# A chunk's products with itself: three split products on the whole array, or float32 products in its four quarters, with one output copied ahead of a cast

## The chip, the cores and the metric

One Trainium2 chip, one core of it. The metric is the device time of one execution in microseconds (us), lower is better. The kernel before took 387.55 us (median of 3 runs, 386.8 to 387.71).

## The reference, cut to what matters

```python
# x (8, 4224, 192), weight (8 heads, 7 taps): a causal convolution in time, heads of 24 channels
w = softmax(weight, axis=-1)
x = sum over k of w[h, k] * x[b, s - 6 + k, head h]       # per head of 24 channels
# then, on its result x, with w_val, w_out (192, 192) and conv_w (5, 192)
gate = sigmoid(sum over k of conv_w[k] * x[b, s - 4 + k])  # per channel
val = x @ w_val
out = (gate * val) @ w_out                                 # float32
```

## The kernel before, in words

Channels lie on the partitions, time along the free axis. The 8 sequences are laid end to end in two streams of four. Of 192 channels 128 form chunk 1 and 64 form chunk 2. Chunk 1 has a plane for each stream (`x1`, two planes of 128 partitions); chunk 2 of both streams shares one plane (`x2`: stream 0 on partitions 0 to 63, stream 1 on 64 to 127). A stream's time is cut into 14 groups and these into 37 steps (`STEPS`): two of 288 columns, six of 432, 27 of 482, and at the end one of 500 and one of 244. A step holds both streams, so its planes have 482 columns each.

**Stage 1, the first convolution** (`conv_unit`, L303). TensorE multiplies windows of `x` with a band matrix of the softmax weights, as float32 products of 64 by 64 (or 56) with 58 columns, four beside each other in the four quarters of the array (L319). Two PSUM outputs `pc` of a unit are copied by ScalarE to `e` (L330), and DMAs of SyncE's queue scatter `e` into `x1` and `x2` (L359). A group has six units in the main part, made two groups ahead, two units a step (`todo`).

**Stage 2, the gate.** ScalarE opens it with the first tap (`gate_open`, L393), VectorE adds four taps (`gate_taps`, L400), ScalarE closes with a sigmoid (`gate_close`, L413); in two parts: A is chunk 1 (`pa`, `g1`), B chunk 2 (`pb`, `g2`).

**Stage 3, the value projection, and stage 4, the output projection.** `v` is `x` times `w_val`; VectorE multiplies it into the gate in place (`gated`, L511); `o` is that product times `w_out`, one step later; ScalarE copies `o` to `ot` (`project`, L527), and a DMA writes it out. A plane is split ahead of its products (`split1`, `split2`): ScalarE casts it to a float32r high part (`xh`, `ph`; L421 for chunk 1, L429 for chunk 2), GpSimd subtracts that for the low part (`xl`, `pl`; L422, L430). A split product is three matmuls: high by high, low weight by high, high weight by low. A projection has four kinds of products, by the chunk that goes in and the chunk that comes out:

- `main` (L464): chunk 1 to chunk 1, per stream three split matmuls of 128 by 128.
- `rows` (L477): chunk 2 to chunk 1, split, for each stream in its 64 rows of the array.
- `columns` (L492): chunk 1 to chunk 2, in float32, 128 by 64, a stream in each half of the array's columns, in four pieces of 120 or 121 columns.
- `diagonal` (L454): chunk 2 to chunk 2. Its weight is a 128 by 128 block with the 64 by 64 weight twice on the diagonal (`W22`), so three split matmuls of all 482 columns take both streams.

The outputs are `v_0`, `v_1` (chunk 1, a plane per stream) and `v_2` (chunk 2 of both), and the same of `o`.

**What sets the order.** The engines run in the order in which the code issues (`manual_schedule`). In the main loop (L640) a step n issues on TensorE: `diagonal` of `v` n and of `o` n-1, `main` of `v`, `columns` of `v` and of `o`, `rows` of `v` and of `o`, `main` of `o`, two conv units. VectorE's order is two A taps, `gated` 2, a B tap, `gated` 0, a B tap, `gated` 1, then A, B, A, B. ScalarE's is close and open B, the split of n+1, close and open A, the cast of chunk 2's gated product, the copy of `o_2`, the cast of chunk 1's gated product (`split_gated1`), the copies of `o_0` and `o_1`, the four copies of the conv units. Steps 0 to 3 have a loop of their own (`HEAD`, L579).

**PSUM.** The gate's `pa` and `pb` hold three of the eight banks. The other five rotate (pool `ps`, five buffers): an output gets the bank of the fifth output before it and waits until that is read. With two conv units a step's ten outputs are, in order, `v_2`, `o_2`, `v_0`, `v_1`, `o_0`, `o_1`, `pc` 0 and 1 of the first unit, `pc` 0 and 1 of the second. So the second unit's `pc` 1 waits for the copy of `o_0`, the next step's `v_2` for the copy of `o_1`, and the next `o_2` for the copy of the first unit's `pc` 0.

Of the kernel before, what the change touches and what calls it, by code (L numbers as in the profile page):

```python
# [44 lines left out]
def second(n):  # L45
    return NS * n * WIN - reach(n)
# [24 lines left out]
STEPS = []  # L71
# [34 lines left out]
def kernel(  # L106
# [9 lines left out]
    nc = tc.nc  # L116
# [18 lines left out]
    o = 0  # L135
# [128 lines left out]
    W11, W12, W21, W22 = 0, 128, D, D + 128  # L264
# [24 lines left out]
    w_val, w_out = Weight("wv"), Weight("wo")  # L289
# [3 lines left out]
    HALVES = (slice(0, 64), slice(64, 128))  # L293
# [80 lines left out]
    def views(n, k=KG - 1):  # L374
        g, o, m = STEPS[n]
        b = second(NJS[g])
        x1v = x1s[g][:, : 2 * b].rearrange("p (a t) -> p a t", a=2)
        return x1v[:, :, o + k : o + k + m], x2s[g][:, o + k : o + k + m]
# [3 lines left out]
    accs, g1s, g2s, xs, pr, ots, banks = {}, {}, {}, {}, {}, {}, {}  # L382
# [12 lines left out]
    def gate_taps(n, i, k0=1, k1=KG):  # L395
        if n >= N:
            return
        acc = accs[n, i]
        for k in range(k0, k1):
            nc.vector.scalar_tensor_tensor(  # L400
                out=acc, in0=views(n, k)[i], scalar=cwt[:, i, k : k + 1],
                in1=acc, op0=ALU.mult, op1=ALU.add,
            )

    def gate_close(n, i):
        if n >= N:
            return
        m = STEPS[n][2]
        if i == 0:
            dst = g1s[n] = gp.tile([128, 2, MB], F32, tag="g1", name=f"g1_{n}")[:, :, :m]  # L410
        else:
            dst = g2s[n] = gp.tile([128, MB], F32, tag="g2", name=f"g2_{n}")[:, :m]
        nc.scalar.activation(dst, accs.pop((n, i)), AF.Sigmoid)  # L413
# [3 lines left out]
    def split1(pool, tag, n, x):  # L417
        m = STEPS[n][2]
        h = pool.tile([128, 2, MB], F32R, tag="h", name=f"{tag}h_{n}")[:, :, :m]
        l = pool.tile([128, 2, MB], F32R, tag="l", name=f"{tag}l_{n}")[:, :, :m]  # L420
        nc.scalar.copy(h, x)  # L421
        nc.gpsimd.tensor_tensor(out=l, in0=x, in1=h.bitcast(F32), op=ALU.subtract)  # L422
        return h, l
# [9 lines left out]
    def bank(what, n, q):  # L433
        t = ps.tile([128, 512], F32, tag="p", name=f"{what}_{n}_{q}")[:, : STEPS[n][2]]
        banks[what, n, q] = t
        return t

    def operands(what, n):
        return (w_val, *xs[n, 1], *xs[n, 2]) if what == "v" else (w_out, *pr[n, 1], *pr[n, 2])

    def parts(w, h, l):
        return (w.h, h), (w.l, h), (w.h, l)

    def ok(n):
        return 0 <= n < N

    def diagonal(what, n):
        if not ok(n):
            return
        acc = bank(what, n, 2)  # L450
        w, _, _, h2, l2 = operands(what, n)
        r = slice(W22, W22 + 128)
        for i, (a, b) in enumerate(parts(w, h2, l2)):
            nc.tensor.matmul(acc, lhsT=a[:, r], rhs=b, start=(i == 0), stop=False)  # L454

    def main(what, n, q):
        if not ok(n):
            return
        fresh = (what, n, q) not in banks
        acc = bank(what, n, q) if fresh else banks[what, n, q]  # L460
        w, h, l, _, _ = operands(what, n)
        r = slice(W11, W11 + 128)
        for i, (a, b) in enumerate(parts(w, h, l)):
            nc.tensor.matmul(  # L464
                acc, lhsT=a[:, r], rhs=b[:, q], start=(fresh and i == 0), stop=(not fresh and i == 2)
            )

    def rows(what, n):
        if not ok(n):
            return  # L470
        fresh = (what, n, 0) not in banks
        two = [bank(what, n, q) if fresh else banks[what, n, q] for q in range(2)]
        w, _, _, h2, l2 = operands(what, n)
        r = slice(W21, W21 + 128)
        for i, (a, b) in enumerate(parts(w, h2, l2)):
            for acc, p in zip(two, HALVES):
                nc.tensor.matmul(  # L477
                    acc, lhsT=a[p, r], rhs=b[p], start=(fresh and i == 0), stop=(not fresh and i == 2)
                )

    def columns(what, n):
        if not ok(n):
            return
        m = STEPS[n][2]
        acc = banks[what, n, 2]
        w = w_val if what == "v" else w_out
        x = views(n)[0] if what == "v" else g1s[n]
        cuts = [m * i // 4 for i in range(5)]
        for i in range(4):
            c = slice(cuts[i], cuts[i + 1])  # L490
            for q, p in enumerate(HALVES):
                nc.tensor.matmul(  # L492
                    acc[p, c], lhsT=w.f[:, W12 : W12 + 64], rhs=x[:, q, c],
                    start=False, stop=(i == 3),
                )

    def split(n):
        if n >= N:
            return
        x1, x2 = views(n)  # L500
        if n < 2:
            xs[n, 2] = split2(sp, "x", n, x2)
        xs[n, 1] = split1(sp, "x", n, x1)
        if n >= 2:
            xs[n, 2] = split2(sp, "x", n, x2)

    def gated(n, q):
        if not ok(n):
            return
        v = g1s[n][:, q] if q < 2 else g2s[n]  # L510
        nc.vector.tensor_tensor(out=v, in0=banks.pop(("v", n, q)), in1=v, op=ALU.mult)  # L511

    def split_gated1(n):
        if ok(n):
            pr[n, 1] = split1(pp, "p", n, g1s[n])

    def split_gated2(n):
        if ok(n):
            pr[n, 2] = split2(pp, "p", n, g2s[n])

    def project(n, q):
        if not ok(n):
            return
        m = STEPS[n][2]
        if n not in ots:
            ots[n] = op.tile([128, 3 * MB], F32, tag="ot", name=f"ot_{n}")
        nc.scalar.copy(ots[n][:, q * m : (q + 1) * m], banks.pop(("o", n, q)))  # L527
        o = 3 * sum(s[2] for s in STEPS[:n])
        if n == LAST:
            nc.sync.dma_start(out[:, o + q * m : o + (q + 1) * m], ots[n][:, q * m : (q + 1) * m])  # L530
        elif q == 1:
            nc.sync.dma_start(out[:, o : o + 3 * m], ots[n][:, : 3 * m])
# [9 lines left out]
    def conv(k):  # L542
        for _ in range(k):
            if done[0] < len(units):
                conv_unit(done[0])
                done[0] += 1

    todo = [0] * (N + 1)
    for g in range(LAG, NG):
        a, b = SOON.get(g) or (first[g - LAG], first[g - 1])  # L550
# [27 lines left out]

    for n in range(HEAD):  # L579
        k = 2 if n < 2 else 3  # L580
        diagonal("v", n)
        split(n + 1)
        if n != 1:
            diagonal("o", n - 1)
        main("v", n, 0)
        main("v", n, 1)
        if n == 1:
            diagonal("o", n - 1)
        else:
            gate_taps(n + 1, 0, 1, k)  # L590
        columns("v", n)
        gated(n, 2)
        if n == 1:
            gate_taps(n + 1, 0, 1, k)
        columns("o", n - 1)
        split_gated2(n)
        project(n - 1, 2)
        rows("v", n)
        gated(n, 0)
        gated(n, 1)  # L600
        rows("o", n - 1)
        main("o", n - 1, 0)
        project(n - 1, 0)
        main("o", n - 1, 1)
        project(n - 1, 1)
        conv(1)
        split_gated1(n)
        now = todo[n] if n == 0 else todo[n] // 2
        conv(now - 1)
        gate_taps(n + 1, 0, k, KG)  # L610
        gate_close(n + 1, 0)
        gate_open(n + 2, 0)
        gate_taps(n + 1, 1)
        conv(todo[n] - now)
        gate_close(n + 1, 1)
        gate_open(n + 2, 1)
# [16 lines left out]
    def flush(i):  # L633
        for n, _ in [p for p in pending if p[1] == i]:
            gate_close(n, i)
            gate_open(n + 1, i)
            pending.remove((n, i))

    taps("AA")
    for n in range(HEAD, N + 1):  # L640
        diagonal("v", n)
        flush(1)
        split(n + 1)
        diagonal("o", n - 1)
        main("v", n, 0)
        main("v", n, 1)
        taps("AA")
        columns("v", n)
        gated(n, 2)
        flush(0)  # L650
        taps("B")
        columns("o", n - 1)
        split_gated2(n)
        project(n - 1, 2)
        rows("v", n)
        gated(n, 0)
        taps("B")
        gated(n, 1)
        rows("o", n - 1)
        split_gated1(n)  # L660
        main("o", n - 1, 0)
        taps("ABAB")
        project(n - 1, 0)
        main("o", n - 1, 1)
        project(n - 1, 1)
        conv(todo[n])
# [77 lines left out]
```

## Time and profile before

| | us |
|---|---|
| median of 3 runs | 387.55 |
| the profiled execution | 383.81 |
| its span, first to last instruction | 382.0 |
| TensorE busy in the span | 356.5 |
| VectorE busy | 331.7 |
| ScalarE busy | 327.6 |
| GpSimd busy | 251.1 |
| TensorE's mean granted clock | 0.996 |

The profile's page gives the busy time of each engine over the span; the views of the trace behind it give single instructions with start, duration and, in brackets, the idle time ahead and what ended it. TensorE's recorded durations include the way through the array, so that neighbours overlap: what a matmul costs is the difference of two starts. A float32 product shows as two records, so 8 products stand as x16. Some matmul records are missing. PE is TensorE, ACT ScalarE, DVE VectorE, POOL GpSimd, SP SyncE.

### The profile page before, as it was taken

The page shows a single profiled execution, that of the slowest core. Times are in us where ns is not written, and L with a number is a line of the kernel's source. Part 1 is how long each engine was busy: PE and PEld are TensorE (multiplying, and loading weights), DVE is VectorE, ACT ScalarE, POOL GpSimd, SP SyncE. Part 2 cuts the span into 40 slices and gives each one's busy share as a digit, 9 for nine tenths or more (in the row PEclk, how much of TensorE's full clock was granted, in tenths as well). Part 3 has the DMA queues.
Part 4 walks back from the last instruction along what each step waited for, and adds up shares of the span by engine and source line. Part 5 has one row for each costly group of instructions (what it writes and reads, how often), then busy time and mean ns, then how long its engine had stood idle before and what let it go on. Part 6 is the DMA issues. An engine that isn't in the chain of part 4 may idle for free.

```text
span 382.0 us, 14551 instructions
## 1 busy us (share of the span) xinstructions
PE 356.5 (93%) x6130; PEld 289.1 (76%) x6130; DVE 331.7 (87%) x439; ACT 327.6 (86%) x570; POOL 251.1 (66%) x177
## 2 busy tenths in 40 slices
PE   8798988898999999999999999999999999999895
PEld 7776876787877777777777777777877777776684
DVE  3899889688998988999898898898898899999960
ACT  7589889879998898898898899899899999898863
POOL 1969655556666666666767766666667666677772
PEclk9899999999999999999999999999999999999999
DMA  8888787996986986986986996996898794431224
GB/s 272 232 250 252 223 284 224 257 266 202 277 266 171 258 273 189 238 264 196 243 262 187 205 270 205 232 288 204 203 272 252 177 297 143 140 114 78 79 104 174
DMA packets 38954, 83.30 MB, mean 218 GB/s; under 512 B 4936, under 2 KB 17008, under 8 KB 38888
## 3 DMA queue, kind: packets, MB, share of 16 engines
q1 hardware_dynamic: 37440, 80.64, 71.4%
q0 software_dynamic: 896, 1.27, 1.4%
q8 instruction: 48, 0.79, 0.9%
q10 hardware_dynamic: 552, 0.46, 0.4%
q14 instruction: 18, 0.15, 0.2%
HBM read 30.06 MB, written 26.00 MB: 147 GB/s over the span
## 4 chain that ended last, share of the span: by engine, by line
PE 43%; DVE 14%; ACT 13%; DMA 12%; POOL 9%; issue 5%; SPq 3%; DVEq 0%; ACTq 0%; POOLq 0%
DMA x<-e 11%; PE v L464 8%; DVE g L511 6%; PE pc L319 6%; ACT ph L421 6%; PE v L492 6%; PE v L477 5%; PE o L492 5%; DVE pb L400 5%; PE v L454 5%; PE o L454 4%; POOL pl L422 4%; ACT ot L527 3%; PE o L464 2%; SPq L359 2%
## 5 line engine op out<-in xcount | busy, mean ns | idle before, releaser
L400 DVE SCALAR_TENSOR_TENSOR pa<-x,cwt,pa 128x964 f32<-128x964 f32 (+4 forms) x148 | 173.2, 1170 | 2.3 <-ACT pa L393 0.4
L422 POOL TENSOR_TENSOR xl<-x,xh 128x964 fp32r<-128x964 f32 (+4 forms) x37 | 73.5, 1987 | 81.5 <-ACT xh L421 70.5
L400 DVE SCALAR_TENSOR_TENSOR pb<-x,cwt,pb 128x482 f32<-128x482 f32 (+4 forms) x148 | 102.4, 692 | 0.6
L422 POOL TENSOR_TENSOR pl<-g,ph 128x964 fp32r<-128x964 f32 (+4 forms) x37 | 79.6, 2152 | 29.1 <-ACT ph L421 25.1
L511 DVE TENSOR_TENSOR g<-v,g 128x482 f32<-128x482 f32 (+4 forms) x111 | 69.5, 631 | 32.8 <-PE v L492 20.0
L319 PE MATMUL pc<-band,x 64*56 64x58 f32 (+1 forms) x3776 | 74.4, 220 | 14.7 <-ACT ot L527 9.1
L319 PEld LDWEIGHTS pc<-band,x 64*56 64x56 f32 (+1 forms) x3776 | 65.3, 132 | 28.1 <-ACT ot L527 13.5
L330 ACT COPY e<-pc 120x348 f32<-120x348 f32 (+2 forms) x148 | 59.5, 489 | 5.1 <-PE pc L319 5.1
L527 ACT COPY ot<-o 128x482 f32<-128x482 f32 (+4 forms) x111 | 56.2, 538 | 3.0 <-PE o L464 2.4
L421 ACT CAST ph<-g 128x964 fp32r<-128x964 f32 (+4 forms) x37 | 35.4, 958 | 23.0 <-DVE g L511 22.8
L430 POOL TENSOR_TENSOR pl<-g,ph 128x482 fp32r<-128x482 f32 (+4 forms) x37 | 43.6, 1179 | 2.7 <-ACT ph L429 2.7
L430 POOL TENSOR_TENSOR xl<-x,xh 128x482 fp32r<-128x482 f32 (+4 forms) x37 | 42.0, 1136 | 3.2 <-ACT xh L429 3.1
L393 ACT ACTIVATE pa<-x,cwt 128x964 f32<-128x964 f32 (+4 forms) x37 | 38.1, 1030 | 2.8 <-DMA x<-e 1.7
L492 PEld LDWEIGHTS v<-x,wvf 128*64 128x64 f32 x592 | 29.3, 136 | 11.7 <-issue 10.8
L492 PE MATMUL v<-x,wvf 128*64 128x121 f32 (+5 forms) x592 | 37.4, 267 | 0.0
L492 PE MATMUL o<-g,wof 128*64 128x121 f32 (+5 forms) x592 | 35.5, 261 | 0.0
L413 ACT ACTIVATE g<-pa 128x964 f32<-128x964 f32 (+4 forms) x37 | 34.3, 927 | 1.2 <-DVE pa L400 1.1
L421 ACT CAST xh<-x 128x964 fp32r<-128x964 f32 (+4 forms) x37 | 34.8, 942 | 0.0
L464 PE MATMUL o<-ph,woh 128*128 128x482 f32 (+4 forms) x74 | 31.2, 421 | 0.0
L492 PEld LDWEIGHTS o<-g,wof 128*64 128x64 f32 x592 | 30.8, 136 | 0.1
L464 PE MATMUL v<-xh,wvh 128*128 128x482 f32 (+4 forms) x74 | 27.5, 372 | 1.2 <-ACT e L330 1.2
L464 PE MATMUL o<-pl,woh 128*128 128x482 f32 (+4 forms) x74 | 27.5, 372 | 0.0
(75 smaller groups left out, 568.8 us busy)
## 6 DMA issues: line engine op xcount, KB each, us to landing
x<-xw SPq DMA_DIRECT2D x72, 300.0 KB
out<-ot SPq DMA_DIRECT2D x27, 723.0 KB
x<-e SPq DMA_DIRECT2D x45, 271.9 KB
x<-xw SPq DMA_DIRECT2D x16, 360.0 KB
x<-e SPq DMA_DIRECT2D x36, 135.9 KB
out<-ot SPq DMA_DIRECT2D x6, 648.0 KB
x<-e SPq DMA_DIRECT2D x20, 163.1 KB
x<-e SPq DMA_DIRECT2D x18, 90.6 KB
```

Of the source, the lines that this page charges most:

```text
L319: nc.tensor.matmul(pc[r][c0:c1, k * HW : (k + 1) * HW], lhsT=xtiles[i][p, c + c0 : c + c1], rhs=band[p, 4 * q + hi, :], start=True, stop=True,
L330: nc.scalar.copy(ev[:, a : a + w, r, :], pc[r][:M, : w * HW].rearrange("p (w t) -> p w t", t=HW))
L393: nc.scalar.mul(acc, views(n, 0)[i], cwt[:, i, 0:1])
L400: nc.vector.scalar_tensor_tensor(out=acc, in0=views(n, k)[i], scalar=cwt[:, i, k : k + 1], in1=acc, op0=ALU.mult, op1=ALU.add,)
L421: nc.scalar.copy(h, x)
L422: nc.gpsimd.tensor_tensor(out=l, in0=x, in1=h.bitcast(F32), op=ALU.subtract)
L430: nc.gpsimd.tensor_tensor(out=l, in0=x, in1=h.bitcast(F32), op=ALU.subtract)
L454: nc.tensor.matmul(acc, lhsT=a[:, r], rhs=b, start=(i == 0), stop=False)
L464: nc.tensor.matmul(acc, lhsT=a[:, r], rhs=b[:, q], start=(fresh and i == 0), stop=(not fresh and i == 2))
L492: nc.tensor.matmul(acc[p, c], lhsT=w.f[:, W12 : W12 + 64], rhs=x[:, q, c], start=False, stop=(i == 3),)
L511: nc.vector.tensor_tensor(out=v, in0=banks.pop(("v", n, q)), in1=v, op=ALU.mult)
L527: nc.scalar.copy(ots[n][:, q * m : (q + 1) * m], banks.pop(("o", n, q)))
```

## The change

`diagonal` is no longer split. It takes the float32 planes themselves (`x2` of step n, and the gated `g2` of step n-1) with the float32 weight's 64 by 64 blocks, in four pieces of 120 or 121 columns, and does `v` of n and `o` of n-1 in one go: for `v` the quarters on the array's diagonal (rows and columns 0 to 63, rows and columns 64 to 127), for `o` the two others, so that `o_2` now has stream 0 on partitions 64 to 127 and stream 1 on 0 to 63. `columns` of `o` and the host's reading of the result follow that exchange. In the main loop the first half of `main` of `o` and the copy of `o_0` are issued ahead of the cast `split_gated1`. In the first four steps step 1 no longer has its `o` diagonal behind `main`, and a step with an odd number of conv units does the larger half first (of these steps that is step 3 alone: two units ahead of the gate's taps instead of one).

```diff
-    def diagonal(what, n):
-        acc = bank(what, n, 2)
-        w, _, _, h2, l2 = operands(what, n)
-        r = slice(W22, W22 + 128)
-        for i, (a, b) in enumerate(parts(w, h2, l2)):
-            nc.tensor.matmul(acc, lhsT=a[:, r], rhs=b, start=(i == 0), stop=False)
+    def diagonal(n):
+        todo = []
+        for what, m in (("v", n), ("o", n - 1)):
+            if ok(m):
+                acc = bank(what, m, 2)
+                w, x = (w_val, views(m)[1]) if what == "v" else (w_out, g2s[m])
+                for r in range(2):
+                    dst = acc[HALVES[r if what == "v" else 1 - r]]
+                    todo.append((dst, w.f[HALVES[r], W22 + 64 * r : W22 + 64 * r + 64], x[HALVES[r]], STEPS[m][2]))
+        for i in range(4):
+            for dst, w, x, m in todo:
+                c = slice(m * i // 4, m * (i + 1) // 4)
+                nc.tensor.matmul(dst[:, c], lhsT=w, rhs=x[:, c], start=(i == 0), stop=False)
...
-                    acc[p, c], lhsT=w.f[:, W12 : W12 + 64], rhs=x[:, q, c],
+                    acc[HALVES[q if what == "v" else 1 - q], c], lhsT=w.f[:, W12 : W12 + 64], rhs=x[:, q, c],
...
-        now = todo[n] if n == 0 else todo[n] // 2
+        now = todo[n] if n == 0 else (todo[n] + 1) // 2
...
     for n in range(HEAD, N + 1):
-        diagonal("v", n)
+        diagonal(n)
         flush(1)
         split(n + 1)
-        diagonal("o", n - 1)
         main("v", n, 0)
...
         rows("o", n - 1)
+        main("o", n - 1, 0)
+        project(n - 1, 0)
         split_gated1(n)
-        main("o", n - 1, 0)
         taps("ABAB")
-        project(n - 1, 0)
         main("o", n - 1, 1)
```

On TensorE, at the start of step 14 of the main loop, there stand before, behind the last conv unit's products, six split matmuls of the diagonal (`xh2`, `xl2` and `ph2`, `pl2` are chunk 2's high and low parts) and then those of `main`:

```order
L319 MATMUL pc_39_1_2845<-band_91,x_47_2548 64x58
L454 MATMUL v_14_2_2878<-xh2_14_2729,wvh_157 128x482
L454 MATMUL v_14_2_2878<-xh2_14_2729,wvl_158 128x482
L454 MATMUL v_14_2_2878<-xl2_14_2730,wvh_157 128x482
L454 MATMUL o_13_2_2894<-ph2_13_2769,woh_161 128x482
L454 MATMUL o_13_2_2894<-ph2_13_2769,wol_162 128x482
L454 MATMUL o_13_2_2894<-pl2_13_2770,woh_161 128x482
L464 MATMUL v_14_0_2898<-xh_14_2725,wvh_157 128x482
```

In the changed kernel the same place has float32 products on the planes themselves (`x2`, `g2`; `wvf` and `wof` are the float32 weights), 16 in all:

```order
L319 MATMUL pc_39_1_2980<-band_91,x_47_2663 64x58
L460 MATMUL v_14_2_3013<-x2_6_2070,wvf_156 64x120 x2
L460 MATMUL o_13_2_3014<-g2_13_2860,wof_160 64x120 x2
L460 MATMUL v_14_2_3013<-x2_6_2070,wvf_156 64x121 x2
L460 MATMUL o_13_2_3014<-g2_13_2860,wof_160 64x121 x2
...
L470 MATMUL v_14_0_3043<-xh_14_2864,wvh_157 128x482
```

Products of `v` and `o` now alternate, and neither needs a high or low part.

On ScalarE, in the same step before, the cast of chunk 1's gated product (`ph_13`) stands ahead of the copies of `o_0` and `o_1` to `ot`:

```order
L527 COPY ot_12_2773<-o_12_2_2733 128x482
L421 CAST ph_13_2792<-g1_13_2591 128x2x482
L527 COPY ot_12_2773<-o_12_0_2784 128x482
L527 COPY ot_12_2773<-o_12_1_2785 128x482
L330 COPY e_7_1_2681<-pc_38_0_2809 120x7x58
```

And in the changed kernel:

```order
L533 COPY ot_12_2908<-o_12_2_2843 128x482
L533 COPY ot_12_2908<-o_12_0_2919 128x482
L421 CAST ph_13_2931<-g1_13_2716 128x2x482
L533 COPY ot_12_2908<-o_12_1_2920 128x482
L330 COPY e_7_1_2806<-pc_38_0_2944 120x7x58
```

The copy of `o_0` has moved ahead of the cast; nothing else on ScalarE has changed places.

More of the change, by code (lines that the diff above doesn't have):

```diff
@@ L445, in ok @@
         return 0 <= n < N
-    def diagonal(what, n):
-        if not ok(n):
-            return
-        acc = bank(what, n, 2)
-        w, _, _, h2, l2 = operands(what, n)
-        r = slice(W22, W22 + 128)
-        for i, (a, b) in enumerate(parts(w, h2, l2)):
-            nc.tensor.matmul(acc, lhsT=a[:, r], rhs=b, start=(i == 0), stop=False)
+    def diagonal(n):
[11 more added lines that the diff above has]
+                nc.tensor.matmul(dst[:, c], lhsT=w, rhs=x[:, c], start=(i == 0), stop=False)
     def main(what, n, q):
@@ L490, in columns @@
             c = slice(cuts[i], cuts[i + 1])
-            for q, p in enumerate(HALVES):
+            for q in range(2):
                 nc.tensor.matmul(
-                    acc[p, c], lhsT=w.f[:, W12 : W12 + 64], rhs=x[:, q, c],
+                    acc[HALVES[q if what == "v" else 1 - q], c], lhsT=w.f[:, W12 : W12 + 64], rhs=x[:, q, c],
                     start=False, stop=(i == 3),
@@ L580 @@
         k = 2 if n < 2 else 3
-        diagonal("v", n)
+        diagonal(n)
         split(n + 1)
-        if n != 1:
-            diagonal("o", n - 1)
         main("v", n, 0)
         main("v", n, 1)
-        if n == 1:
-            diagonal("o", n - 1)
-        else:
+        if n != 1:
             gate_taps(n + 1, 0, 1, k)
@@ L640 @@
     for n in range(HEAD, N + 1):
-        diagonal("v", n)
+        diagonal(n)
         flush(1)
         split(n + 1)
-        diagonal("o", n - 1)
         main("v", n, 0)
@@ L741 @@
             full[i, a : a + m, perm[:128]] = blk[:, i]
-            full[i, a : a + m, perm[128:]] = blk[64 * i : 64 * i + 64, 2]
+            full[i, a : a + m, perm[128:]] = blk[64 * (1 - i) : 64 * (1 - i) + 64, 2]
     return np.ascontiguousarray(full.reshape(B, PADB, D)[:, :S])
```

## The prediction

> **What bounds the kernel now.** I read the page first, then the busy time by stretches, TensorE's, ScalarE's and VectorE's timelines of one step, the waits and the chain. The page:
>
> ```profile
> span 382.0 us, 14551 instructions
> PE 356.5 (93%) x6130; PEld 289.1 (76%) x6130; DVE 331.7 (87%) x439; ACT 327.6 (86%) x570; POOL 251.1 (66%) x177
> ```
>
> Three engines are near full. The chain of waits gives the pace: the start of a step's `main` of `v`, 15 steps apart,
>
> ```profile
> 150.03 1.31 PE v L464 x6
> ...
> 299.89 1.32 PE v L464 x6
> ```
>
> (299.89 - 150.03) / 15 = 9.99 us a step. Steps 8 to 29, which are 22, are of this kind: 482 columns, two conv units. One such step on TensorE (start, duration, instruction, and in brackets the idle time ahead):
>
> ```profile
> 204.52 0.48 PE L464 MATMUL o<-ph,woh 128*128 128x482 f32 x1
> ...
> 205.06 0.38 PE L464 MATMUL o<-pl,woh 128*128 128x482 f32 x1
> ...
> 206.02 1.02 PE L319 MATMUL pc<-band,x 64*64 64x58 f32 x50
> 207.43 1.03 PE L319 MATMUL pc<-band,x 64*56 64x58 f32 x54 [0.39 <-ACT ot L527]
> 208.40 0.49 PE L454 MATMUL v<-xh,wvh 128*128 128x482 f32 x1
> 208.72 0.38 PE L454 MATMUL v<-xh,wvl 128*128 128x482 f32 x1
> ...
> 209.82 0.38 PE L464 MATMUL v<-xh,wvh 128*128 128x482 f32 x1
> ...
> 211.23 1.05 PE L492 MATMUL v<-x,wvf 128*64 128x120 f32 x16
> 212.10 1.00 PE L492 MATMUL o<-g,wof 128*64 128x120 f32 x16
> 213.03 0.49 PE L477 MATMUL v<-xh,wvh 64*128 64x482 f32 x2
> ...
> 214.55 0.48 PE L464 MATMUL o<-ph,woh 128*128 128x482 f32 x1
> ```
>
> TensorE stops once, ahead of the second conv unit, until ScalarE has copied `o_0`. ScalarE over the same step:
>
> ```profile
> 205.92 1.00 ACT L421 CAST ph<-g 128x964 fp32r<-128x964 f32 x1 [0.88 <-DVE g L511]
> 206.82 1.02 ACT L527 COPY ot<-o 128x482 f32<-128x482 f32 x2
> 207.73 1.62 ACT L330 COPY e<-pc 120x348 f32<-120x348 f32 x4
> 209.44 0.57 ACT L413 ACTIVATE g<-pb 128x482 f32<-128x482 f32 x1
> ...
> 214.52 0.56 ACT L527 COPY ot<-o 128x482 f32<-128x482 f32 x1
> 215.96 1.00 ACT L421 CAST ph<-g 128x964 fp32r<-128x964 f32 x1 [0.88 <-DVE g L511]
> ```
>
> It waits 0.88 us for VectorE's last `gated`, casts, and only then copies `o_0`. VectorE:
>
> ```profile
> 204.03 0.66 DVE L511 TENSOR_TENSOR g<-v,g 128x482 f32<-128x482 f32 x1 [0.34 <-PE v L477]
> ...
> 205.23 0.66 DVE L511 TENSOR_TENSOR g<-v,g 128x482 f32<-128x482 f32 x1
> ...
> 208.69 0.72 DVE L400 SCALAR_TENSOR_TENSOR pb<-x,cwt,pb 128x482 f32<-128x482 f32 x1
> ...
> 214.07 0.66 DVE L511 TENSOR_TENSOR g<-v,g 128x482 f32<-128x482 f32 x1 [0.36 <-PE v L477]
> ```
>
> So the pace is a loop through three engines: `rows` of `v` (one step ahead of the row at 213.03) to `gated` 0 and 1, to ScalarE's cast at 205.92, to the copy of `o_0` ending at 206.82 + 0.56, to the second conv unit at 207.43, to `diagonal` at 208.40, `main`, `columns`, and `rows` again at 213.03. Any gain must shorten this loop, and what is next late matters as much as what is saved.
>
> **The diagonal.** It now costs 209.82 - 208.40 = 1.42 us a step: six split matmuls at 0.22 ((209.82 - 208.72) / 5), and 0.10 because the first after a change of tiling takes 0.32 (208.72 - 208.40). The new one is 16 float32 products of 120 or 121 columns. The row nearest to it is `columns` of `o`: eight products of that size, in the two halves of the array's columns, from 212.10 to 213.03, 0.93 us with the change of tiling behind it. If all four quarters run beside each other, 16 take the same 0.93. That they can, conv units show: 28 products of 58 columns in at most the 1.02 us of the row at 206.02, though in pairs at the rate of `columns` they would need 14 x 0.93 / 4 x 58 / 120.5 = 1.57. `main` behind it now pays the 0.10. From the diagonal's start to `columns` that makes 0.93 + 0.10 + (211.23 - 209.82 = 1.41) = 2.44, against 211.23 - 208.40 = 2.83 before: 0.39 saved a step. That no change of tiling is left between conv units and the diagonal may save up to another 0.10; I leave it in the range. Nothing waits for more than before: `x2` was landed for the split a step earlier, `g2` was multiplied a step earlier, and the low parts (`xl2`, `pl2`) are now needed only at `rows`, later. What is new is that the first `o` product, and all behind it, wait for `o_2`'s bank, that is for the copy of the first conv unit's `pc` 0, at the diagonal's start and not 0.7 us later. That is in the loop below.
>
> A rule speaks against it. The Trainium skill, TensorEngine Tiling (Array Packing), section "Restrictions and Gotchas", says that different row tiles cannot access the same PSUM bank simultaneously; here stream 0 (rows 0 to 63) and stream 1 (rows 64 to 127) of `v` both write `v_2`'s bank. By that rule the block would take turns, and the time would be that of the second rival. No row of this trace shows two row tiles in one bank, so it can neither be confirmed nor refuted here.
>
> **The eviction ahead of the cast.** ScalarE's work is the same. `o_0` is complete after three matmuls, 205.06 + 0.38 = 205.44, inside ScalarE's 0.88 us of idle time, so the copy moves into it and the second conv unit no longer waits. The cast can become late by a copy, 0.46 ((207.73 - 206.82) / 2); GpSimd, which makes the low part from it, is idle a third of the time (row of stretches below), and the reader of both, the next step's `main` of `o`, comes 8.6 us after the cast began (214.55 - 205.92), which covers it. No queue of DMAs is passed: the DMA of `ot` hangs on the copy of `o_1`, still behind the cast.
>
> **The new pace.** From the start P of the cast: cast 0.90 (206.82 - 205.92), copy of `o_1` 0.46, first copy of a conv output some 0.45 (1.62 / 4, and its end), 0.05 as from copy to conv unit (207.38 to 207.43): the diagonal at P + 1.86. Then 2.44 to `columns`, 1.80 to `rows` (213.03 - 211.23), 1.52 to `main` of `o` (214.55 - 213.03), 0.92 until `o_0` is complete (205.44 - 204.52), 0.05, and its copy 0.46: the next cast at P + 9.05. Over VectorE the cast is free at nearly the same point: `rows` + 1.04 (214.07 - 213.03) + 1.20 (205.23 - 204.03) + 0.69 (205.92 - 205.23) is P + 9.03.
> A second loop runs over two steps. ScalarE's next sigmoid needs the last B tap, 4.21 after `gated` 1 starts (209.44 - 205.23), in the new order too, since VectorE's taps are not moved; from it to the copy of `o_2` are 5.08 (214.52 - 209.44), that and the copy of `o_0` 0.48 + 0.46, then the cast: 10.23 after `gated` 1, which starts at P + 1.86 + 2.44 + 1.80 + 1.04 + 1.20 = P + 8.34. So the cast after next is not ahead of P + 18.57, 9.29 a step. The longer one sets the pace: 9.29, a saving of 0.70 x 22 = 15.4 us. Under it lie ScalarE alone (215.96 - 205.92 - 0.88 = 9.16) and VectorE alone, which the last steps, without conv units, show with no idle time:
>
> ```profile
> 331.47 0.65 DVE L511 TENSOR_TENSOR g<-v,g 128x482 f32<-128x482 f32 x1
> ...
> 340.33 0.65 DVE L511 TENSOR_TENSOR g<-v,g 128x482 f32<-128x482 f32 x1
> ```
>
> 8.86 a step. So the last steps gain nothing, and 9.16 is the best for the others: 18.3 us.
>
> The first eight steps are held up by other things as well, such as a scatter that lands late:
>
> ```profile
> 85.32 1.07 ACT L393 ACTIVATE pa<-x,cwt 128x964 f32<-128x964 f32 x1 [1.68 <-DMA x<-e]
> ```
>
> Where the diagonal's `o` half waits there for a bank, main products no longer start behind a finished `v` half alone; the unit that step 3 issues earlier puts two copies of 0.45 ahead of a sigmoid. For these eight steps I take a gain between -1 us (such a delay in one step) and +3 (8 x 0.39), and of it +0.7, about half of the diagonal's 0.39 in steps 4 to 7.
> Sum: 382.0 - 15.4 - 0.7 = 365.9 us of span. The profiled execution took 383.81, 1.81 more than its span, so 367.7, a ratio of 0.958. The runs' median is 387.55: 0.958 x 387.55 = 371.3 us.
>
> **The rivals.**
> *DMA becomes the limit.* The stretch from 150 to 180 us (busy us of PE, PEld, DVE, ACT, POOL, then the clock, the DMA engines' busy share and GB/s):
>
> ```profile
> 150.00:180.00 30.00, 29.08 (x508) 23.35 (x507) 27.09 (x34) 27.12 (x46) 19.95 (x12) 1.00 0.84 234
> ```
>
> 0.84 would be 0.90 at 9.29 us. If loads and scatters then come late, as at 85.32, I take half of the gain as lost: 387.55 - 8 = 379.5. Against it: two groups of lead, and no wait for a DMA in the quoted step.
> *The streams take turns*, because both write one bank: the block takes 0.83 more than forecast (0.93 without its 0.10 change of tiling). The first loop is then 9.05 + 0.83 = 9.88, the second 18.57 + 0.83 = 19.40 or 9.70 a step: 9.88, saving 0.11 x 22 = 2.4 us, 385 us. (The rule of the Trainium skill named above would have it so.) Against it: in `columns` the two halves of the partitions of one bank are written in turns of 0.93 / 4, too short for eight products one by one (twice that); but those are column tiles of all 128 rows, and no row shows two row tiles in one bank.
> *Slower: the four quarters take turns one by one*, since neighbours in issue order share a bank, a row tile or a column tile. The block is 4 x 0.83 + 0.10 = 3.42, the first loop 9.05 + 3.42 - 0.93 = 11.54, 1.55 x 22 = 34 us longer: 421 us. It decides from a block of 0.93 + (9.99 - 9.05) = 1.87 us on. The conv units, whose four quarters overlap, speak against it.
>
> **How the numbers follow.** About 0.3% (1.2 us) is what a measurement of this kernel can tell from no change. The forecast has 0.76 (its own range 366 to 377: 9.16 a step and 2 us more in the first steps at one end, 9.5 a step at the other), the DMA limit 0.09, turns by two 0.10, turns one by one 0.05. Faster takes the first two and half of the third: 0.90; no change 0.05; slower 0.05. The range, 366 to 380, holds the first two cases.
>
> **What would show it.** Right: diagonal to `main` in about 0.93 us with `v` and `o` records starting within a few ns of each other; no wait of conv units for `ot`; the copy of `o_0` between 0.5 us and no time ahead of the cast; VectorE's waits for `v` L492 and L477 nearly gone; 9.2 to 9.4 us between steps. Wrong: a block of 1.7 us or more (turns), waits on `x<-e` or `x<-xw` in the main steps (DMA), or a pace still near 10 with a new wait of the diagonal for `e`, which would say that ScalarE's order holds the loop.

## The result, and the profile after

The changed kernel took 374.68 us (median of 4 runs, 370.65 to 379.15) against 387.18 before; the ratio is 0.966, 95% interval 0.956 to 0.976: faster, inside the range of 366 to 380, 3.4 us above the 371.3 forecast. A second timing, last among the experiments, gave 0.971 (0.966 to 0.977). The profiled execution took 374.82 us. Ratios here and below leave out executions over 1.5% longer than the fastest of their kernel, here the one of 379.15 us, and in the experiments two of 515 and 404 us (8 and 9) at granted clocks of 0.56 and 0.75 among others.

The page after, with the row of the queue that brings instructions (packets, MB, share):

```profile
span 373.0 us, 16456 instructions
PE 344.0 (92%) x7092; PEld 277.1 (74%) x7092; DVE 330.7 (89%) x439; ACT 325.9 (87%) x570; POOL 250.3 (67%) x177
q8 instruction: 56, 0.92, 1.1%
```

VectorE and ScalarE do what they did, in 9 us less; TensorE has 962 more matmul records and is busy 12.5 us less. One main step on TensorE:

```profile
198.48 1.05 PE L498 MATMUL v<-x,wvf 128*64 128x120 f32 x16
...
203.30 1.74 PE L319 MATMUL pc<-band,x 64*64 64x58 f32 x104
204.90 0.42 PE L460 MATMUL v<-x,wvf 64*64 64x120 f32 x4
205.25 0.32 PE L460 MATMUL o<-g,wof 64*64 64x120 f32 x2
...
205.92 0.37 PE L460 MATMUL o<-g,wof 64*64 64x121 f32 x4
206.23 0.49 PE L470 MATMUL v<-xh,wvh 128*128 128x482 f32 x1
...
207.73 1.05 PE L498 MATMUL v<-x,wvf 128*64 128x120 f32 x16
...
217.05 1.05 PE L498 MATMUL v<-x,wvf 128*64 128x120 f32 x16
```

The conv units are one run of 104 records with no wait in it, and the diagonal follows. Its first four `v` records start at once, then it holds until 205.25, and `o` and `v` run side by side to `main` at 206.23: 0.98 us. (`main` comes 1.33 us after the diagonal's first record.) From 198.48 to 217.05 are two steps: 18.57 us. ScalarE in the same step:

```profile
202.47 1.01 ACT L533 COPY ot<-o 128x482 f32<-128x482 f32 x2
203.38 1.00 ACT L421 CAST ph<-g 128x964 fp32r<-128x964 f32 x1
204.27 0.57 ACT L533 COPY ot<-o 128x482 f32<-128x482 f32 x1
204.73 1.62 ACT L330 COPY e<-pc 120x348 f32<-120x348 f32 x4
206.65 0.58 ACT L413 ACTIVATE g<-pb 128x482 f32<-128x482 f32 x1 [0.30 <-DVE pb L400]
```

The idle 0.88 us ahead of the cast is gone: `o_2` and `o_0` are copied together and the cast follows directly. The first of the four copies of `pc`, from 204.73, is what the diagonal's `o` products waited for until 205.25, which is 1.87 us after the cast began; the forecast had 1.86. And a wait that is new: the sigmoid on B, 0.30 us, for VectorE's last B tap. VectorE's own waits for `v` (L498 and L483, the L492 and L477 of before) are less than half of before, 8.8 us between 95 and 318 us against 20.1, but not nearly gone, as the prediction had listed.

Not forecast at all are waits inside TensorE's runs that the trace puts down to nothing it shows ("issue"), and a late start:

```profile
20.41 3.12 PE L319 MATMUL pc<-band,x 64*64 64x58 f32 x95 [4.26 <-DMA x<-xw]
...
302.25 0.47 PE L498 MATMUL v<-x,wvf 128*64 128x120 f32 x5 [0.84 <-issue]
...
309.25 0.31 PE L319 MATMUL pc<-band,x 64*64 64x58 f32 x6 [1.26 <-issue]
```

The 309.25 wait stands in the middle of a conv unit whose inputs have long been there.

Where the 9.0 us of span came from, by the first record of `columns` of `v` in steps 0, 8 and 30: before

```profile
22.43 0.72 PE L492 MATMUL v<-x,wvf 128*64 128x72 f32 x16
...
101.42 0.32 PE L492 MATMUL v<-x,wvf 128*64 128x120 f32 x2
...
320.97 0.33 PE L492 MATMUL v<-x,wvf 128*64 128x120 f32 x2
```

and after

```profile
26.16 0.31 PE L498 MATMUL v<-x,wvf 128*64 128x72 f32 x2
...
103.17 0.32 PE L498 MATMUL v<-x,wvf 128*64 128x120 f32 x2
...
311.84 0.32 PE L498 MATMUL v<-x,wvf 128*64 128x120 f32 x2
```

Step 0 came 3.7 us later, steps 0 to 7 were 2.0 us shorter, steps 8 to 29 took 208.7 us instead of 219.6, and the rest was the same (61.1 us before, 61.2 after). 22 steps of 9.28 would be 204.2: steps 8 to 29 lost 4.5 us to waits.

### The profile page after: what moved, and what is told of

Same layout as the page of the kernel before. It is cut to its first block, busy times and chain, and to the rows that moved or that the text cites. A ratio compares the mean times of both kernels' runs of the same rounds, so it can differ in the third digit from the quotient of the medians.

```text
span 373.0 us, 16456 instructions
## 1 busy us (share of the span) xinstructions
PE 344.0 (92%) x7092; PEld 277.1 (74%) x7092; DVE 330.7 (89%) x439; ACT 325.9 (87%) x570; POOL 250.3 (67%) x177
## 3 DMA queue, kind: packets, MB, share of 16 engines
q0 software_dynamic: 896, 1.27, 1.4%
## 4 chain that ended last, share of the span: by engine, by line
PE 64%; DVE 13%; ACT 11%; DMA 6%; issue 4%; SPq 1%; ACTq 0%; DVEq 0%
PE pc L319 12%; PE v L470 11%; PE o L470 10%; PE v L498 7%; DVE pa L400 6%; PE v L483 6%; PE o L498 6%; PE o L460 5%; PE o L483 5%; DVE pb L400 4%; PE v L460 3%; DMA x<-e 3%; DVE g L517 2%; ACT e L330 2%; DMA x<-xw 2%
## 5 line engine op out<-in xcount | busy, mean ns | idle before, releaser
L422 POOL TENSOR_TENSOR pl<-g,ph 128x964 fp32r<-128x964 f32 (+4 forms) x37 | 79.3, 2142 | 24.1 <-ACT ph L421 15.4
L319 PEld LDWEIGHTS pc<-band,x 64*56 64x56 f32 (+1 forms) x3776 | 61.3, 132 | 22.3 <-issue 9.4
L319 PE MATMUL pc<-band,x 64*64 64x58 f32 (+1 forms) x3776 | 67.3, 221 | 10.1 <-DMA x<-xw 4.5
L533 ACT COPY ot<-o 128x482 f32<-128x482 f32 (+4 forms) x111 | 57.6, 541 | 7.8 <-PE o L470 7.2
L460 PE MATMUL v<-x,wvf 64*64 64x121 f32 (+5 forms) x592 | 41.6, 268 | 2.4 <-ACT g L413 2.0
L460 PE MATMUL o<-g,wof 64*64 64x121 f32 (+5 forms) x592 | 37.8, 263 | 3.1 <-issue 1.7
L498 PEld LDWEIGHTS v<-x,wvf 128*64 128x64 f32 x592 | 29.3, 136 | 13.5 <-issue 11.7
L498 PE MATMUL v<-x,wvf 128*64 128x121 f32 (+5 forms) x592 | 37.7, 268 | 1.5 <-issue 1.5
L498 PE MATMUL o<-g,wof 128*64 128x121 f32 (+5 forms) x592 | 35.8, 261 | 0.1
L460 PEld LDWEIGHTS o<-g,wof 64*64 64x64 f32 x592 | 29.5, 133 | 6.5 <-ACT e L330 3.8
L460 PEld LDWEIGHTS v<-x,wvf 64*64 64x64 f32 x592 | 30.6, 135 | 4.8 <-ACT g L413 2.1
```

What stands on the lines that cost most here:

```text
L319: nc.tensor.matmul(pc[r][c0:c1, k * HW : (k + 1) * HW], lhsT=xtiles[i][p, c + c0 : c + c1], rhs=band[p, 4 * q + hi, :], start=True, stop=True,
L460: nc.tensor.matmul(dst[:, c], lhsT=w, rhs=x[:, c], start=(i == 0), stop=False)
L498: nc.tensor.matmul(acc[HALVES[q if what == "v" else 1 - q], c], lhsT=w.f[:, W12 : W12 + 64], rhs=x[:, q, c], start=False, stop=(i == 3),)
```

## The experiments

Each ratio is to the kernel before, run on the same chip, with its 95% interval. "Undisturbed" is the mean step among steps 8 to 29 that hold no wait called issue (neighbours taken in pairs, since many kernels alternate); "lost" is what steps 8 to 29 took beyond 22 of those, in the one profiled execution; in two by two (381.99 us) and the change again (378.28 us) that is the longest of the kernel's runs. How steps are picked moves the "undisturbed" of kernels with many such waits by some hundredths.

| kernel | matmul records | undisturbed, us | lost, us | ratio |
|---|---|---|---|---|
| before | 6130 | 9.98 | 0 | 1 |
| the change | 7092 | 9.28 | 4.5 | 0.966 (0.956 to 0.976) |
| diagonal alone | 7092 | 9.52 | 6.8 | 0.984 (0.977 to 0.991) |
| order alone | 6130 | 9.35 | 0 | 0.967 (0.962 to 0.972) |
| diagonal in one piece | 6204 | 9.26 | 0.5 | 0.961 (0.955 to 0.966) |
| B taps first | 7092 | 9.28 | 8.5 | 0.976 (0.969 to 0.984) |
| eight pieces | 8276 | 9.33 | 27 | 1.051 (1.046 to 1.057) |
| two by two | 7092 | 9.35 | 12 | 0.978 (0.971 to 0.984) |
| one piece, taps early | 6204 | 9.15 | 0 | 0.949 (0.944 to 0.954) |
| one piece, columns too | 5316 | 9.24 | 0 | 0.953 (0.949 to 0.958) |
| pieces and taps | 5316 | 9.13 | 0.3 | 0.950 (0.945 to 0.954) |
| order, taps early | 6130 | 9.35 | 0 | 0.963 (0.960 to 0.967) |
| the change again | 7092 | 9.28 | 8.6 | 0.971 (0.966 to 0.977) |

**1. The diagonal alone.** The order of the kernel before is restored:

```diff
+        split_gated1(n)
         main("o", n - 1, 0)
-        project(n - 1, 0)
-        split_gated1(n)
         taps("ABAB")
+        project(n - 1, 0)
```

> The float32 diagonal in four quarters, but the cast ahead of the copy of o_0 as before the change. Theory (the pace is the longest loop): the second conv unit waits again for the copy of o_0, 1.55 us after the cast starts, so the diagonal comes 2.5 us after the cast instead of 1.9; 9.65 us a step instead of the 9.29 of the whole change (9.99 before), some 8 us longer than the whole change, about 0.980 of before. Rival (the order does everything, the diagonal is hidden): 9.99 a step, the time of before. Rival (TensorE's own work is the limit, the order does nothing): 9.3 a step, the time of the whole change.

Measured: 9.52 us a step where undisturbed, 0.13 less than expected:

```profile
220.87 1.05 PE L498 MATMUL v<-x,wvf 128*64 128x120 f32 x16
...
227.03 0.97 PE L319 MATMUL pc<-band,x 64*56 64x58 f32 x53 [0.20 <-ACT ot L533]
...
230.39 1.05 PE L498 MATMUL v<-x,wvf 128*64 128x120 f32 x16
```

The wait for the copy of `o_0` is back. Both rivals fall: the pace is neither 9.98 nor 9.28. Of the 10.1 us that the better pace would bring (0.46 x 22), the profiled execution lost 6.8 to the new waits.

**2. The order alone.** The same lines moved in the kernel before, its split diagonal kept.

> The split diagonal of before, and only the copy of o_0 (with its half of main) moved ahead of the cast. Theory: both loops grow by the 0.39 us of the longer block against the whole change: 9.44 and (18.57 + 0.39) / 2 = 9.48, so 9.48 us a step, 0.51 x 22 = 11 us faster than before, about 0.971. Rival (the order does everything): 9.3 a step, the time of the whole change, 0.964. Rival (TensorE's own work is the limit): 9.6 to 10 a step, since TensorE's work stays, between 0.975 and 1.

Measured: 9.35 and 0.967, the whole change's ratio without its diagonal, and nearest to the rival in which the order does everything. It is under the 9.48 of my own loops, and why stands in its timeline:

```profile
199.61 1.74 PE L319 MATMUL pc<-band,x 64*64 64x58 f32 x104
201.28 0.48 PE L454 MATMUL v<-xh,wvh 128*128 128x482 f32 x1
...
202.03 0.38 PE L454 MATMUL o<-ph,woh 128*128 128x482 f32 x1
...
202.70 0.38 PE L464 MATMUL v<-xh,wvh 128*128 128x482 f32 x1
...
204.09 1.05 PE L492 MATMUL v<-x,wvf 128*64 128x120 f32 x16
```

No row has a bracket. That alone shows little, since in the changed kernel the diagonal holds without one (204.90 to 205.25). But the same steps of 9.31 and 9.44, by whether the units hold 13 or 14 windows, come back in experiment 10 under another order on VectorE; so I take 9.35 for TensorE's own work. The split `v` half runs, from 201.28, while `o_2`'s bank is still being copied out (ScalarE's cast started at 199.58 here; + 1.86 is 201.44), and only the 0.67 us of the `o` half (202.70 - 202.03) stand behind the bank. In the quarters, all but the first few products stand behind it: 0.98. So in the loop through the bank the new block is no shorter than the old one; what it does is free TensorE's time.

**3. The diagonal in one piece.** Four products of 482 columns instead of 16 of 120 or 121:

```diff
-        for i in range(4):
+        for i in range(1):
             for dst, w, x, m in todo:
-                c = slice(m * i // 4, m * (i + 1) // 4)
+                c = slice(0, m)
```

> The changed kernel with each diagonal product in one piece of 482 columns instead of four pieces: 4 products instead of 16 a step, 48 TensorE instructions fewer (weight loads among them), the same columns streamed. Theory (the waits that the trace calls issue inside runs of conv units, 0.4 to 1.7 us in six places and some 6 us in all, are TensorE waiting for its instruction stream, which the change made longer): with 6091 - 4 x 37 x 6 or so fewer records they fall back to the one or two of before, a pace of 9.3 us a step stays, and the time is 2 to 5 us under the changed kernel's. Rival (these waits are chance, or belong to DMA traffic): as many of them, and the same time within 1 us. If one piece keeps the four quarters from overlapping, the block is 1.7 us or more, and the pace 9.8.

(The count in it is garbled: it is 24 records a step fewer, 7092 - 24 x 37 = 6204.) Measured: no wait called issue over 0.3 us in steps 8 to 29, 9.26, and 0.961, 2 us under the change's first ratio, which lies inside that one's interval, and 4 us under its second. The quarters overlap in one piece as in four: from the first `o` record to `main` 0.96 us, against 0.97 (medians of 22 steps).

**4. B taps first.** `taps("BABA")` for `taps("ABAB")`.

> The changed kernel with VectorE's last four taps of a step in the order B, A, B, A instead of A, B, A, B. The last B tap then ends 1.13 us earlier, and ScalarE's sigmoid on B can start earlier by that. Theory (the second loop, from the last B tap over ScalarE's row of work to the cast, holds the pace at 9.29): that loop shrinks to 17.4 over two steps, and what remains is the first loop of 9.05 and ScalarE's own 9.16; 9.15 to 9.2 us a step, 2 to 3 us less than the changed kernel; ScalarE's wait of 0.3 us for the B tap is gone. Rival (TensorE alone holds the pace, its loop of 9.2 to 9.3 with no free time): 9.27 a step, the same time.

A miss: 9.28, as without it. The sigmoid on B waits no more, but now the sigmoid on A does, in half of the steps:

```profile
152.65 0.98 ACT L413 ACTIVATE g<-pa 128x964 f32<-128x964 f32 x1 [0.47 <-DVE pa L400]
```

The last A tap ends a step's chain on VectorE in either order; in the changed kernel it was 0.2 us from binding (A's last tap ended at 209.00, the sigmoid began at 209.24, in the step shown). I freed one of two waits that were nearly equal. That the loop runs over VectorE's taps this does not refute, nor show.

**5. Eight pieces.** `range(8)` and eighths for `range(4)` and quarters.

> The changed kernel with each diagonal product in eight pieces of 60 or 61 columns instead of four: 128 more TensorE instructions a step (weight loads among them), the same columns. Theory (TensorE runs out of instructions where many short ones stand together, as one piece took the waits called issue from 6.3 to 2.7 us in all and the four pieces of the first experiment had 9.2): these waits grow to 15 us or more and the time with them, 385 us or more; the steps without such a wait keep 9.3 to 9.4 us. Rival (chance or DMA): waits as with four pieces, 3 to 10 us, and a time within 3 us of the changed kernel's.

Measured: 404.41 us, 16 waits called issue over 0.3 us in steps 8 to 29, the longest 2.47 us. The diagonal stalls in its own middle:

```profile
183.98 0.30 PE L460 MATMUL o<-g,wof 64*64 64x60 f32 x2 [2.47 <-issue]
```

The instruction queue of this kernel, and of the one in one piece:

```profile
q8 instruction: 65, 1.06, 1.1%
```

```profile
q8 instruction: 49, 0.80, 0.9%
```

With the same columns streamed, 49, 56 and 65 packets of instructions go with 0.5, 4.5 and 27 us lost. The rival (chance or DMA alone) falls. No view names a packet as the releaser, but the traces hold the times of the packets and show it. A packet has 16,384 bytes, and the change's 56 packets go with 14,184 matmuls and weight loads, 253 each. Over all thirteen profiles 80 waits called issue are longer than 0.3 us. Counted over TensorE's records, every one of them ends at the same place in a block of 256 (record 193 or 194, from 0), and 1.17 to 1.73 us after a packet has landed. The packet ahead of the wait shown landed at 182.42. So TensorE waits for its instructions.

**6. Two by two.** The two quarters of `v`, all pieces, and then those of `o`:

```diff
-        for i in range(4):
-            for dst, w, x, m in todo:
+        for part in (todo[:2], todo[2:]):
+            for i in range(4):
+                for dst, w, x, m in part:
```

> The changed kernel with the two quarters of v first, all four pieces, and the two of o behind them: the quarters no longer four at a time. This is the price of the rival in which the quarters take turns by two. Theory: a block of 0.82 + 0.93 = 1.75 us or so instead of 0.98; the wait for the bank of o_2 falls into the v half; TensorE's own work, 9.35 us a step with the split diagonal of 1.42, becomes 9.35 + 1.75 - 1.42 = 9.7, and that is the pace, 0.4 x 22 = 9 us longer than the changed kernel. Rival (the pace is ScalarE's and VectorE's, TensorE has time left): 9.3 a step, no longer than the changed kernel.

```profile
217.68 0.73 PE L461 MATMUL v<-x,wvf 64*64 64x120 f32 x10
218.15 0.32 PE L461 MATMUL o<-g,wof 64*64 64x120 f32 x2
...
218.45 0.27 PE L461 MATMUL v<-x,wvf 64*64 64x121 f32 x2
...
219.13 0.48 PE L471 MATMUL v<-xh,wvh 128*128 128x482 f32 x1
```

The block is 1.45 us, not 1.75: `o`, issued behind all of `v`, starts at 218.15 in its own quarters while the last records of `v` start as late as 218.45. So 1.75 was never tried, and the pace is 9.35 and not 9.7. It fits TensorE's own work all the same: 9.35 with a block of 1.42, and 1.45 here.

**7. One piece, and taps early.** On experiment 3, VectorE's second B tap moves ahead of `gated` 0:

```diff
         gated(n, 2)
         flush(0)
-        taps("B")
+        taps("BB")
...
         gated(n, 0)
-        taps("B")
         gated(n, 1)
```

> One piece as in the third experiment (9.26 a step), and VectorE's second B tap ahead of gated 0 instead of between gated 0 and gated 1: gated 0 waits for TensorE there anyway, so gated 1 starts some 0.4 us earlier against TensorE's rows. Theory (two steps are held by the loop from gated 1 over four taps to ScalarE's sigmoid, ScalarE's row of work to the cast, and the first copy of a conv output to the diagonal): the loop shrinks from 18.57 to 18.2 over two steps, and ScalarE's own 9.16 is next: 9.15 to 9.2 a step, about 2 us less than one piece alone. Rival (TensorE's own work holds the pace): 9.26 a step, the same time.

Measured: 9.15, and 0.949. VectorE's two B taps and then its two `gated` in one run, and TensorE's step:

```profile
192.60 1.47 DVE L400 SCALAR_TENSOR_TENSOR pb<-x,cwt,pb 128x482 f32<-128x482 f32 x2
193.98 1.22 DVE L517 TENSOR_TENSOR g<-v,g 128x482 f32<-128x482 f32 x2
```

```profile
190.82 1.05 PE L498 MATMUL v<-x,wvf 128*64 128x120 f32 x16
...
199.90 1.05 PE L498 MATMUL v<-x,wvf 128*64 128x120 f32 x16
```

(This step took 9.08; neighbours alternate around 9.15.) TensorE's work is that of experiment 3, only VectorE's order differs, and the step is 0.11 shorter: there the loop over the taps held the pace, and TensorE did not.

**8. One piece in `columns` too.** `cuts = [0, m]`, one pass of the loop.

> One piece in the diagonal as in the third experiment, and one piece of 482 columns in the columns products too: 4 products a step there instead of 16, 48 more TensorE instructions fewer. Theory (instruction stream): the waits called issue inside runs fall from 2.7 us to 2 or less, the columns blocks stay at 0.88 and 0.93 us, 9.26 a step, and the time is 0 to 2 us under one piece in the diagonal alone. Rival (pieces are needed for the two halves to overlap): a columns block of 1.6 us or more and a pace above 10.

Measured: no such wait over 0.3 us in steps 8 to 29, 9.24 a step; pieces are not needed for the halves to overlap.

**9. Pieces and taps.** 7 and 8 together.

> What helped, together: one piece in the diagonal and in the columns products, and two B taps ahead of gated 0. Theory: 9.15 us a step as with the taps moved and the diagonal in one piece, no wait called issue inside the main steps; as fast as that kernel or up to 1 us faster, 0.946 to 0.950 of before. Rival (pieces of the columns products matter by themselves): 1.5 us or more either way.

Measured: 0.950 and 9.13, the same as 7 within the interval. Versions 7 and 9 beat both kernels; against the changed kernel's two timings that is 1.7 to 2.3%. On the same chip as experiment 11, the runs behind the ratios took 362.5 to 366.6 us here and 369.9 to 374.3 there.

**10. The order and the taps, with the split diagonal.**

> The split diagonal of before with the copy of o_0 ahead of the cast, and two B taps ahead of gated 0. Theory (with the split diagonal TensorE's own work, 9.35 us a step, is the limit and the loop over the taps lies under it): the taps change nothing here, 9.35 a step, 0.967 as with the order alone; the quarters, which free TensorE, are worth 0.2 us a step once the taps are moved (9.15) and 0.07 before (9.28). Rival (the taps help whatever the diagonal): 9.2 a step, 0.96.

Measured: 9.35 a step, as with the order alone, so there the taps do nothing and TensorE is the limit; the ratio of 0.963 lies between the two expectations, and its interval holds 0.967 at its edge. The two pairs together: with the taps in place the quarters take the step from 9.35 to 9.15, without them from 9.35 to 9.26 or 9.28.

**11. The change again.**

> The changed kernel once more, unaltered, beside the two others on the same chip. Theory: undisturbed steps of 9.28 us in the mean, a different number of waits called issue (4 to 10 us in all) at other places than in its first profile, and a ratio of 0.960 to 0.970 to before. Rival (the two long steps and the late start of the first profile belong to the change): the first columns again at 26 us and waits at the same steps.

Measured: undisturbed steps of 9.28, the first `columns` at 24.1 us, nine waits called issue over 0.3 us in the whole span, and 0.971, a little over the upper end expected. The places are not all others: of the six such waits of the first profile four come back at the same record, one of them under another name. In the first profile and in this one it reads

```profile
161.04 1.05 PE L498 MATMUL v<-x,wvf 128*64 128x120 f32 x16 [0.67 <-issue]
```

```profile
161.12 1.05 PE L498 MATMUL v<-x,wvf 128*64 128x120 f32 x16 [0.86 <-DMA x<-xw]
```

Both end at the place in a block of 256 named in experiment 5, 1.37 and 1.46 us after a packet, so the DMA of `x` is not the cause. The rival's "waits at the same steps" is half right. In the five profiles of 7092 records, steps 8 to 29 have 28 such waits (two of them put down to that DMA), and they stand at only ten of the 34 places where a new block of 256 begins.

Over all profiles of this study step 0's `columns` begin between 21.4 us (order and taps) and 26.2 (the first profile of the change); the kernel with the diagonal alone has 22.1, and the three with the split diagonal 21.4 to 22.7. So the late start does not come with the change each time; whether the change makes one likelier is not shown.

## Why the prediction was right, and where it was not

*The pace.* Forecast 9.29 a step from two loops, measured 9.28, with 18.57 us over two steps to the hundredth. The new wait stands where the second loop has it (the sigmoid on B, 0.30 us, and 0.47 on A once B was freed). That this loop and not TensorE was the limit is shown by moving the taps: 9.26 to 9.15, next to ScalarE's own 9.16, forecast as the floor. It is shown with the diagonal in one piece; with four pieces, which keep the same pace within 0.02, it is inferred. That the forecast meets the measured pace to 0.01 is partly luck: the part from the end of the bank's wait to `columns` took 2.48 us (207.73 - 205.25) against 2.44, so others must have come out as much shorter.

*The block.* Forecast 0.93, measured 0.98 from the end of the bank's wait, with two of the 16 products started before it; the four quarters overlap, also when two of them write one bank. (In experiment 6 the 16 records of `v`, which all write one bank, start between 217.68 and 218.45.) The rule of the Trainium skill (TensorEngine Tiling (Array Packing), section "Restrictions and Gotchas") that different row tiles cannot access one PSUM bank simultaneously did not cost the turns that I priced from it: 0.98 is well under 1.76. Here they write different partitions of the bank. The two rivals of turns fall with that.

*What the diagonal is worth.* Here a step of the prediction failed, without showing in its total. It said "0.39 saved a step" for the path from the diagonal to `columns`. In the loop through `o_2`'s bank nothing of it is saved: the split `v` half had been running during the wait, and the quarters stand behind it. The saving is TensorE's time, 9.35 a step of its own work without it, and lies under the taps' loop but for 0.07. So beside the order the diagonal adds little: 0.63 of 0.70 us a step (9.98 to 9.35) come with the order alone. That is not to say that it is worth nothing by itself: in the old order, where the diagonal stands behind the second conv unit and the wait for `o_0`'s copy, it alone brings 0.46 (9.98 to 9.52). The two gains overlap and do not add up. The prediction had the copy of `o_0` as a wait removed, and that part was right; it did not work out each part alone, which would have shown this.

*What was left out.* The prediction costed the new products by the columns they stream and not by their number. With 962 more records TensorE waited for its instructions, and steps 8 to 29 lost 4.5 and 8.6 us in two profiles (some 0.8 of the 8.6 in a step with a late scatter, shown below). That is the larger part of the gap from 365.9 us of span to 373.0: 4.5 there and 3.7 of a start that varies from run to run, less 1.3 more than forecast in the first eight steps. In steps 8 to 29 the change gave 10.9 us where 15.4 were forecast.

*The other rivals.* DMA did not set the pace: no wait for a scatter in the main steps of the first profile, and 9.15 a step went through as well. In the second profile (experiment 11) ScalarE waits for one, in a step of 10.05 us:

```profile
232.56 1.07 ACT L393 ACTIVATE pa<-x,cwt 128x964 f32<-128x964 f32 x1 [0.70 <-DMA x<-e]
```

*Still open.* Why a packet of instructions comes when it does, and so which of the ten places waits in a given run. The packets ahead of the 42 waits called issue in steps 8 to 29 took 0.90 to 1.35 us, median 1.15, as the others did (medians of 1.04 to 1.14 by kernel): they were not slow on the way, but late to start for what TensorE had left. Whether other DMA traffic delays that start was not tried.

## What to carry to other kernels

Draw the loops and not the engines: with three engines near full, a shorter block on one of them pays only if it lies on the loop that holds the pace, and freeing one of two nearly equal waits shows nothing. A copy that frees a bank belongs ahead of work whose reader comes late, above all where the engine stands idle anyway. Split work into as few instructions as the overlap needs; pieces that cost no columns can still cost time.

## What the runs showed of the hardware that was not expected

- TensorE ran short of instructions: 6204 matmul records or fewer, no wait called issue over 0.3 us in steps 8 to 29; 7092 records, three to six of 0.3 to 2 us; 8276 records, 16 of up to 2.47 us. All end at one place in each block of 256 records, 1.27 to 1.73 us after a packet of instructions landed. A wait of this kind can be put down to a DMA by the trace (0.86 us at 161.12 in experiment 11), or show no gap (the 0.5 us of experiment 3 lie at such a place, at 286.92).
- Products in different quarters of the array overlap out of the order of issue: `o`, issued behind all 16 records of `v`, started before the last of these (218.15 against 218.45).
- One float32 product of 482 columns in a quarter costs no more than four of 120 or 121: 0.96 us against 0.97 from the first `o` record to `main`.
